# Seven chained block products for x @ w1 and x @ w2 in place of seven for the output, in a fused attention and feed-forward kernel on one core

## The chip, the core and the metric

The kernel runs on one core of a Trainium2 chip. The metric is the device time of one execution in microseconds (us). Engines: TensorE (PE; its weight loads are PEld) multiplies matrices from SBUF into PSUM, which has eight banks of 128 x 512 float32; VectorE (DVE), ScalarE (ACT) and GpSimd (POOL) work on elements; SP only issues DMAs. POOL issues DMAs too.

## The reference

Attention in linear form (8 batches, 8 heads, 576 tokens, head size 64), and its output, as x of 4608 tokens by 512, goes through a multiplicative feed-forward network:

```python
def phi(x, c, s):
    r = np.maximum(x, 0.0)
    return np.concatenate([r * c, r * s], axis=-1)
q_p = phi(q, cos_w, sin_w)
k_p = phi(k, cos_w, sin_w)
kv = np.einsum('bhsf,bhsd->bhfd', k_p, v)
num = np.einsum('bhsf,bhfd->bhsd', q_p, kv)
den = np.einsum('bhsf,bhf->bhs', q_p, np.sum(k_p, axis=2))[..., None] + 1e-06
x = (num / den).transpose(0, 2, 1, 3).reshape(4608, 512)
a = x @ w1          # 512 x 1024
b = x @ w2          # 512 x 1024
h = a * b @ w3      # 1024 x 1024
return h @ w_out    # 1024 x 512
```

w3 @ w_out is formed once on the chip (w34b, 1024 x 512), so each token needs x @ w1, x @ w2, the product a*b and (a*b) @ w34. All products are in bfloat16 with float32 sums.

## The kernel before

The order of everything is written out by hand. PLAN is a string of steps, one line for one step of the feed-forward network and what goes with it: "f t" advances tile t (512 tokens; nine of them) by one step, "k b c", "q b c" and "v b c" make the features and values of chunk c of batch b, "kv b" multiplies keys by values, "n b c" the numerators, "d b c" divides (norm), "xd" and "qd" are DMA transposes on SP's queue, the "l..." steps are loads on POOL's queue (some behind a gate, a one-column copy on POOL that waits for a named result), "st" and "ss" are output stores on POOL's and SP's queues. Each engine works through its own instructions in the order of the plan; a scheduler does not move them.

In a feed-forward tile (ffn_groups) TensorE forms a bank of x @ w1 (L702), ScalarE casts it to asb (L745, L762), TensorE forms the bank of x @ w2, and VectorE multiplies the two into abT (L752, L768). That is 64 matmuls of 512 columns, or twice as many of 256 where a tile goes by halves (BY_HALF). There are four PSUM banks for the network, handed out by turns by a pool, and two more ("more") shortly before the end; the others belong to attention.

Tiles 2 to 7 (SEVEN) form their output (a*b) @ w34 as seven block products in place of eight (seven_products, L895): abT is split in 2 x 2 blocks of 256 tokens by 512 columns and w34 in 2 x 2 blocks. VectorE makes sums of abT blocks (sums, L875) and, once, of weight blocks (weight_block, step "tw"), and additions of the products (L903); ScalarE copies two of them (L914, L917). Tile 8 does this for half of its tokens (small_products), tiles 0 and 1 form the output whole. Outputs wait in twelve buffers of 128 x 2 x 512 for their store.

## Time and profile before

| | |
|---|---|
| times of three runs | 242.2, 242.9, 244.04 us; median 242.9 |
| span of the profiled execution, first to last instruction | 240.1 us (its time with what lies around the span is not given apart) |
| TensorE busy, share | 232.5 us, 97% |
| weight loads busy | 163.0 us, 68% |
| VectorE, ScalarE, POOL busy | 190.8, 115.9, 81.9 us |
| granted TensorE clock | 1.00 throughout |
| moved by DMA | 40.48 MB, mean 169 GB/s |

The span is what the profiler records between the first and the last instruction of one execution; the times are of other executions and include what lies before and after, so they are compared with each other, and spans with spans. A busy TensorE is not one at its peak, since matmuls overlap: the mean of one is 379 ns for 512 columns, where four start within 0.86 us. The page lists for each group of instructions the line, the engine, the names out<-in, the shape, the count, then the busy time and the mean of one.

### The profile page before, as it was taken

How to read it: one execution, taken by the hardware profiler on the slowest of the kernel's cores; microseconds unless marked ns; L12 is line 12 of the kernel's file. 1: busy time of each engine (PE TensorE's matmuls, PEld its weight loads, DVE VectorE, ACT ScalarE, POOL GpSimd, SP SyncE). 2: the span in 40 equal slices, each digit the busy share in tenths (PEclk: the TensorE clock that was granted, in tenths of full speed). 3: DMA queues.
4: the chain of work that ended last, by engine and by line, in shares of the span. 5: the costliest groups of instructions: out<-in, count | busy, mean ns of one | idle time of the engine just before them, and what ended most of it. 6: DMA issues, size and time to landing. Idle time of an engine off the chain costs nothing.

```text
span 240.1 us, 5794 instructions
## 1 busy us (share of the span) xinstructions
PE 232.5 (97%) x2216; PEld 163.0 (68%) x2236; DVE 190.8 (79%) x461; ACT 115.9 (48%) x204; POOL 81.9 (34%) x151
## 2 busy tenths in 40 slices
PE   8899999999999999999999999999999999999993
PEld 3579545567965595798589859966995798484462
DVE  6974586968978947999799889998999788785460
ACT  2853304787755732776384437447164312313321
POOL 8744887761803231221430222021020050372020
PEclk9999999999999999999999999999999999999999
DMA  6999999999999999799999999788456938599924
GB/s 191 197 197 199 187 193 184 199 192 195 186 168 141 145 153 212 99 180 184 164 176 172 143 155 168 128 130 84 77 199 129 115 81 156 127 298 308 278 80 176
DMA packets 85995, 40.48 MB, mean 169 GB/s; under 512 B 49616, under 2 KB 83152, under 8 KB 85968
## 3 DMA queue, kind: packets, MB, share of 16 engines
q0 software_dynamic: 38672, 23.60, 66.9%
q1 hardware_dynamic: 47152, 16.46, 40.7%
q8 instruction: 17, 0.28, 0.5%
q14 instruction: 10, 0.08, 0.1%
q10 hardware_dynamic: 144, 0.07, 0.1%
HBM read 38.80 MB, written 9.44 MB: 201 GB/s over the span
## 4 chain that ended last, share of the span: by engine, by line
PE 92%; DMA 3%; POOL 1%; issue 1%; ACT 1%; DVE 1%; POOLq 0%; DVEq 0%
PE ffnps L702 52%; PE ffnps L895 14%; PE ffnps L785 6%; PE ffnps L498 6%; PE pnum L612 4%; PE pnum L577 4%; DMA vs<-in_v_dram 3%; PE ffnmore L895 1%; PE pst L594 1%; PE ffnps L828 1%; PE ffnps L803 1%; PE pst L654 1%; POOL kf L390 1%; PE pnum L973 0%; ACT qpT L598 0%
## 5 line engine op out<-in xcount | busy, mean ns | idle before, releaser
L702 PE MATMUL ffnps<-xT,w2b 128*128 128x256 bf16 (+2 forms) x448 | 76.2, 303 | 0.1
L702 PE MATMUL ffnps<-xT,w1b 128*128 128x256 bf16 (+2 forms) x435 | 75.1, 301 | 0.7
L702 PEld LDWEIGHTS <-w1b 128*128 128x128 bf16 x448 | 41.1, 98 | 19.3 <-issue 0.8
L702 PEld LDWEIGHTS <-w2b 128*128 128x128 bf16 x448 | 40.7, 98 | 19.7 <-issue 0.2
L762 ACT CAST asb<-ffnps 128x512 bf16<-128x512 f32 x40 | 23.4, 586 | 43.2 <-PE ffnps L702 39.3
L768 DVE TENSOR_TENSOR abT<-asb,ffnps 128x512 bf16<-128x512 bf16 x40 | 27.2, 683 | 15.1 <-PE ffnps L702 14.7
L745 ACT CAST asb<-ffnps 128x512 bf16<-128x512 f32 x24 | 14.1, 586 | 32.9 <-PE ffnps L702 25.9
L625 DVE TENSOR_TENSOR xblk<-pnum,den 128x512 bf16<-128x512 f32 (+1 forms) x38 | 26.2, 691 | 1.5
L526 ACT ACTIVATE kp<-kf,sinv 128x512 bf16<-128x512 bf16 (+4 forms) x33 | 21.0, 663 | 0.9 <-DMA kf<-in_k_dram 0.9
L752 DVE TENSOR_TENSOR abT<-asb,ffnps 128x512 bf16<-128x512 bf16 x24 | 16.2, 681 | 6.5 <-PE ffnps L702 6.5
L895 PEld LDWEIGHTS <-abT 128*128 128x128 bf16 x192 | 18.5, 98 | 3.2
L526 ACT ACTIVATE qp<-qs,sinv 128x512 bf16<-128x512 bf16 (+6 forms) x31 | 18.8, 631 | 2.8 <-DMA qpT<-qp 1.2
L441 POOL COPY seen<-asb 128x1 bf16<-128x1 bf16 x15 | 2.9, 191 | 50.1 <-ACT asb L745 45.3
L612 PEld LDWEIGHTS <-qpT 128*128 128x128 bf16 x320 | 15.0, 98 | 4.6 <-DVE xblk L625 0.6
L785 PE MATMUL ffnps<-w34b,abT 128*128 128x512 bf16 x68 | 16.8, 379 | 0.2
L612 PE MATMUL pnum<-kvs,qpT 128*128 128x65 bf16 x304 | 15.7, 194 | 0.2
L895 PEld LDWEIGHTS <-s 128*128 128x128 bf16 x144 | 14.0, 98 | 1.6
L521 DVE TENSOR_SCALAR kp<-kf,cosv 128x512 bf16<-128x512 bf16 (+1 forms) x40 | 14.8, 391 | 0.2 <-DMA kf<-in_k_dram 0.2
L498 PE MATMUL ffnps<-early,w3T 128*128 128x512 bf16 x62 | 14.2, 379 | 0.1
L521 DVE TENSOR_SCALAR qp<-qs,cosv 128x512 bf16<-128x512 bf16 (+1 forms) x34 | 12.7, 384 | 0.3 <-DMA qs<-in_q_dram 0.2
L895 PE MATMUL ffnps<-w34b,abT 128*128 128x256 bf16 x96 | 12.4, 273 | 0.0
L488 DVE STREAM_TRANSPOSE w3T<-early 128x512 bf16<-128x512 bf16 (+1 forms) x12 | 9.9, 864 | 3.0 <-DMA early<-in_moe_w_dram 3.0
(149 smaller groups left out, 336.6 us busy)
## 6 DMA issues: line engine op xcount, KB each, us to landing
out_dram<-osb SPq DMA_DIRECT2D x9, 256.0 KB, 3.4
kf<-in_k_dram POOLq DMA_DIRECT2D x7, 320.0 KB, 7.8
early<-in_moe_w_dram POOLq DMA_DIRECT2D x16, 128.0 KB, 5.1
vs<-in_v_dram POOLq DMA_DIRECT2D x6, 320.0 KB, 7.2
kf<-in_k_dram POOLq DMA_DIRECT2D x7, 256.0 KB, 8.5
qs<-in_q_dram POOLq DMA_DIRECT2D x5, 320.0 KB, 6.7
qs<-in_q_dram POOLq DMA_DIRECT2D x6, 256.0 KB, 6.3
vs<-in_v_dram POOLq DMA_DIRECT2D x6, 256.0 KB, 8.1
```

The source lines that it names most:

```text
L498: nc.tensor.matmul(acc[:, :], lhsT=w3T[:, lc, :], rhs=woutb[:, lc, :], start=(lc == 0), stop=(lc == 7))
L521: nc.vector.tensor_scalar(out=dst[:R, c, :, 0:D], in0=rows[:R], scalar1=0.0, scalar2=cosv[:R, at:at + 1], op0=ALU.max, op1=ALU.mult)
L526: nc.scalar.activation(out=dst[:R, c, 0:n, D:F], in_=rows[:R, 0:n], func=ACTF.Relu, scale=sinv[:R, at:at + 1], bias=0.0)
L612: nc.tensor.matmul(nt[:, h // 4, ds((h % 4) * 65, 65)], lhsT=qpT[:, h, ds(at, 128)], rhs=kvs[:, h, :], start=True, stop=True)
L625: nc.vector.tensor_tensor(out=xblk[rows, g0:g0 + ng], in0=n4[:, :, :, 0:D], in1=den[rows, 0:ng].unsqueeze(3).to_broadcast([R, ng, 4, D]), ...
L702: nc.tensor.matmul(out, lhsT=w[:, kc, ts(jc, 128)], rhs=x[:, kc, tok], start=(kc == 0), stop=(kc == 3))
L745: nc.scalar.copy(out=asb[:], in_=aT[:, :])
L752: nc.vector.tensor_mul(out=abT[:, ts(pair, 2), ts(half, 256)], in0=asb[:].rearrange("p (i n) -> p i n", i=2), in1=bT[:, :].rearrange("p (i ...
L762: nc.scalar.copy(out=asb[:], in_=aT[:, :])
L768: nc.vector.tensor_mul(out=abT[:, jc, :], in0=asb[:], in1=bT[:, :])
L785: nc.tensor.matmul(ops[:, :], lhsT=abT[:, jc, ts(ms, 128)], rhs=w34b[:, jc, :], start=(jc == 0), stop=(jc == 7))
L895: nc.tensor.matmul(into[:, ts(ms, 256)], lhsT=a[:, kc, ts(ms, 128)], rhs=b[:, kc, :], start=(ms == 0 and kc == 0), stop=(ms == 1 and kc == 3))
```

## The change

The seven products move from the output to the front of the tile. In tiles 3 to 8 (FAST) x @ w1 and x @ w2 are taken together as one product of a 2 x 2 block matrix (x split in two blocks of 256 tokens by two of 256 columns) and a 2 x 2 block matrix (rows 0 to 255 and 256 to 511 of w1 and w2). A pass handles 512 of the 1024 columns, in units u of two column blocks; a tile has two passes of seven products, each on two banks (fast_units, step). Products are chained: 1, 6, 5 and 3 go into one bank x[u] one after the other, 7 and 4 into one bank z[u], and between them ScalarE copies the sum so far out (m1, u1, m7, c12) or VectorE adds to it on its way out (c21, c22). Product 2 has a bank of its own (c11). The blocks c11 to c22 are a and b, and the steps "h" multiply them in bfloat16 into the hidden tile. VectorE forms four sums of x blocks a tile ("xs") and, once, four sums of weights ("tf"); the third overwrites part of w2, so no tile after 2 could use w2 as it was.

The output of all tiles is formed whole (whole_out); in fast tiles it is a generator of its own with steps "o", which the plan sets between the "f" steps of the next tile. Banks are handed out by an explicit list, with six for the network from tile 3 on (more_banks moves up; attention keeps one pair). There are nine output buffers in place of twelve, and tile 2 goes whole. All steps of PLAN stand anew: tiles 3 to 8, and in smaller measure the loads, features and copies of attention.

```diff
-MORE = 8
+MORE = 5
-f 3; k 4 4; k 4 2
 ...
+o 2; xs 3 1 V; v 4 0 A; k 4 1 8; xs 3 3 V
+o 2; qd 4 4
+f 3; tf 1 V; d 3 3; tf 3 V; v 5 1 G; qd 4 3; tf 2 V; more; qd 4 2; xs 3 2 V; v 5 2 G; tf 4 V; lt 5 q 1; xs 3 4 V
 ...
-SEVEN = (2, 3, 4, 5, 6, 7)
-BY_HALF = {t: (1, 0) if t == 3 else (0, 1) for t in range(2, 8)}
-ON_POOL = (8,)
+FAST = (3, 4, 5, 6, 7, 8)
+BY_HALF = {2: (0, 1)}
 ...
+    parts = const.tile([P, 6, 512], FP32, name="parts")
+    sides = const.tile([P, 8, 512], BF16, name="sides")
 ...
     def ffn_tile():
-        return ffn_pool[0].tile([P, 512], FP32, name="ffnps")
+        free.append(free[0])
+        return free.pop(0)
+
+    def keep_bank():
+        return free.pop(0)
 ...
+    W11, W12, W21, W22 = (w[:, ts(r, 2), :] for r in range(2) for w in (w1b, w2b))
 ...
+    def ffn_weight_sum(i, on):
+        t1, t2, t3, t4 = wsum
+        out, a, b = ((t1, W12, W11), (t2, W22, t1), (t3, W22, W12), (t4, W21, t2))[i - 1]
+        on.tensor_tensor(out=out, in0=a, in1=b, op=ALU.subtract)
 ...
+    def x_sum(t, i, on):
+        s1, s2, s3, s4 = xsums
+        a11, a12, a21, a22 = (x_block(t, r, c) for r in range(2) for c in range(2))
+        out, a, b, op = ((s1, a21, a22, ALU.add), (s2, s1, a11, ALU.subtract), (s3, a11, a21, ALU.subtract),
+                         (s4, a12, s2, ALU.subtract))[i - 1]
+        on.tensor_tensor(out=out, in0=a, in1=b, op=op)
+
+    def fast_units(t):
+        (s1, s2, s3, s4), (t1, t2, t3, t4) = xsums, wsum
+        a11, a12, a21, a22 = (x_block(t, r, c) for r in range(2) for c in range(2))
+        factors = {1: (W11, a11), 2: (W21, a12), 3: (W22, s4), 4: (t4, a22), 5: (t1, s1), 6: (t2, s2), 7: (t3, s3)}
+        abT = h_of[t] = Hidden(t)
+        m7, u1, m1 = (parts[:, ts(i, 2)] for i in range(3))
+        c11, c12, c21, c22 = (sides[:, ts(i, 2)] for i in range(4))
+        x, z = {}, {}
+
+        def product(into, u, m, first=True):
+            w, a = factors[m]
+            for i in range(2):
+                for kc in range(2):
+                    nc.tensor.matmul(into[:, ts(i, 256)], lhsT=w[:, kc, ts(2 * u + i, 128)], rhs=a[:, kc, :],
+                                     start=(first and i == 0 and kc == 0), stop=(i == 1 and kc == 1),
+                                     skip_group_check=not first)
+
+        def step(p, m):
+            for j in range(2):
+                u = 2 * p + j
+                if m == 1:
+                    x[u] = keep_bank()
+                    product(x[u], u, 1)
+                    nc.scalar.copy(out=m1[:, j], in_=x[u][:, :])
+                    newest[0] = m1[:, j]
+                elif m == 7:
+                    z[u] = keep_bank()
+                    product(z[u], u, 7)
+                    nc.scalar.copy(out=m7[:, j], in_=z[u][:, :])
+                elif m == 6:
+                    product(x[u], u, 6, False)
+                    nc.scalar.copy(out=u1[:, j], in_=x[u][:, :])
+                elif m == 4:
+                    product(z[u], u, 4, False)
+                    nc.vector.tensor_tensor(out=c21[:, j], in0=z[u][:, :], in1=u1[:, j], op=ALU.add)
+                    free.append(z[u])
+                elif m == 2:
+                    y = ffn_tile()
+                    product(y, u, 2)
+                    nc.vector.tensor_tensor(out=c11[:, j], in0=y[:, :], in1=m1[:, j], op=ALU.add)
+                elif m == 5:
+                    product(x[u], u, 5, False)
+                    nc.vector.tensor_tensor(out=c22[:, j], in0=x[u][:, :], in1=m7[:, j], op=ALU.add)
+                elif m == 3:
+                    product(x[u], u, 3, False)
+                    nc.scalar.copy(out=c12[:, j], in_=x[u][:, :])
+                    free.append(x[u])
+
+        def combine(p, r, on):
+            a, b = ((c11, c12), (c21, c22))[r]
+            on.tensor_mul(out=abT.at(4 * p, 4, ts(r, 256)), in0=a.rearrange("p n (i m) -> p (n i) m", i=2),
+                                 in1=b.rearrange("p n (i m) -> p (n i) m", i=2))
+
+        finish[t] = combine
+        for p, m in ((0, 1), (0, 7), (0, 6), (0, 4), (0, 2), (0, 5), (1, 1), (1, 7), (0, 3), (1, 6), (1, 4), (1, 2), (1, 5), (1, 3)):
+            step(p, m)
+            yield
```

What the change does to the order shows best on three engines. On VectorE, before, the additions of an output (L903) in a tile with attention between them; osb and s are output and side buffers, qp and kp features, den and xblk the division:

```order
L903 TENSOR_TENSOR osb_83<-ffnps,osb_82 128x2x256
L903 TENSOR_TENSOR s_1478<-ffnps,osb_83 128x512
L521 TENSOR_SCALAR qp_93<-qs,cosv 128x8x64
L903 TENSOR_TENSOR osb_82<-ffnps,osb_82 128x2x256
L903 TENSOR_TENSOR s_1479<-osb_83 128x512
L903 TENSOR_TENSOR osb_83<-ffnps,s_1479 128x2x256
L903 TENSOR_TENSOR osb_82<-ffnps,s_1478 128x2x256
L903 TENSOR_TENSOR osb_83<-osb_83,s_1478 128x2x256
```

On VectorE now, the first pass of tile 4, with the additions of products 4 (L896), 2 (L901) and 5 (L904), each for two banks, and the two products of a and b (L912):

```order
L896 TENSOR_TENSOR sides<-ffnps_409,parts 128x512
L896 TENSOR_TENSOR sides<-ffnps_408,parts 128x512
L510 TENSOR_SCALAR qp_92<-qs,cosv 128x8x64
L618 TENSOR_SCALAR den<-pnum 128x8
L619 RECIPROCAL den<-den 128x8
L620 TENSOR_TENSOR xblk<-pnum,den 128x512
L901 TENSOR_TENSOR sides<-ffnps_407,parts 128x512
L901 TENSOR_TENSOR sides<-ffnps_409,parts 128x512
L904 TENSOR_TENSOR sides<-ffnmore_1702,parts 128x512
L904 TENSOR_TENSOR sides<-ffnmore_1703,parts 128x512
```

Before, TensorE waited for such an addition only when the bank came round again; now product 3 goes into the very banks that the last two rows read.

On ScalarE, before, a stretch of one tile, where four casts in a row serve four banks and the features stand between tiles:

```order
L526 ACTIVATE qp_93<-qs,sinv 128x8x64
L762 CAST asb<-ffnps 128x512 x4
L526 ACTIVATE kp_92<-kf,sinv 64x8x64
L914 COPY osb_86<-ffnps 128x2x256
L917 COPY osb_87<-ffnps 128x2x256
L542 COPY va_94<-vs 128x8x64
```

On ScalarE now, the first pass of tile 5: the copies of products 1 (L885), 7 (L890) and 6 (L893), the copy of keys by values (kvs), and features of batches 7 and 6 behind them:

```order
L885 COPY parts<-ffnps_408 128x512
L885 COPY parts<-ffnps_407 128x512
L576 CAST kvs<-pnum 128x520
L890 COPY parts<-ffnps_409 128x512
L890 COPY parts<-ffnps_410 128x512
L893 COPY parts<-ffnps_408 128x512
L893 COPY parts<-ffnps_407 128x512
L515 ACTIVATE kp_91<-kf,sinv 128x6x64
L515 ACTIVATE kp_91<-kf,sinv 128x4x64
L515 ACTIVATE qp_92<-qs,sinv 128x8x64
L515 ACTIVATE qp_92<-qs,sinv 64x4x64
L885 COPY parts<-ffnps_409 128x512
```

The last row is the second pass's product 1: a feature that waits for its load holds it. Every copy of product 1, 7 and 6 is now waited for by a later product into the same bank.

At the seam between tile 2 and tile 3, VectorE now has the sums of x blocks (L859) and of weights (L844) with a division between them, ahead of the first additions:

```order
L859 TENSOR_TENSOR early<-xT 128x512
L510 TENSOR_SCALAR kp_91<-kf,cosv 128x8x64
L859 TENSOR_TENSOR early<-xT 128x512
L844 TENSOR_TENSOR turned<-w2b,w1b 128x2048
L618 TENSOR_SCALAR den<-pnum 128x8
L619 RECIPROCAL den<-den 128x8
L620 TENSOR_TENSOR xblk<-pnum,den 128x512
L844 TENSOR_TENSOR w2b<-w2b 128x2048
L844 TENSOR_TENSOR turned<-w2b,turned 128x2048
L859 TENSOR_TENSOR early<-early,xT 128x512
L844 TENSOR_TENSOR early<-w1b,turned 128x2048
L859 TENSOR_TENSOR early<-xT,early 128x512
```

Before, the weight sums of the old scheme (step "tw") stood one by one in tiles 1 and 2.

More of the change, by code (lines that the diff above doesn't have):

```diff
@@ L697, in new_abT @@
         def new_abT():
[L698 removed]
+            h_of[t] = Hidden(t)
+            return h_of[t]
         def products(out, w, jc, tok):
@@ L724, in on_half @@
                             yield
[L725 to L726 removed]
+                asb = next_side()
+                nc.scalar.copy(out=asb, in_=a[:, :])
                 newest[0] = asb
[L728 to L729 removed]
+                nc.vector.tensor_mul(out=abT.at(2 * pair, 2, ts(half, 256)),
+                                     in0=asb.rearrange("p (i n) -> p i n", i=2),
                                      in1=b[:, :].rearrange("p (i n) -> p i n", i=2))
                 yield
[L733 to L734 removed]
+        if t in FAST:
+            yield from fast_units(t)
+            return
         if t <= 1:
@@ L797, in ffn_groups @@
-        if small:
-            for at, n, copy, queue in ((0, 384, nc.scalar.copy, nc.sync),
-                                       (384, 128, nc.vector.tensor_copy, nc.scalar)):
-                cols = ds(at, n)
-                ops = ffn_tile()
-                for jc in range(8):
-                    nc.tensor.matmul(ops[:, 0:n], lhsT=abT[:, jc, ts(3, 128)],
-                                     rhs=w34b[:, jc, cols], start=(jc == 0), stop=(jc == 7))
-                copy(out=osb[:, 1, cols], in_=ops[:, 0:n])
-                store(queue, osb[:, 1:2, :], 4 * t + 3, 1, cols)
-                yield
```

602 lines of the change are left out of this document (251 added, 351 removed).

## The prediction

> **What bounds the kernel now.** I read the page's engine table first, then the chain that ended last, then the waits of TensorE alone, then the windows of the middle tiles.
>
> ```profile
> span 240.1 us, 5794 instructions
> PE 232.5 (97%) x2216; PEld 163.0 (68%) x2236; DVE 190.8 (79%) x461; ACT 115.9 (48%) x204; POOL 81.9 (34%) x151
> PE 92%; DMA 3%; POOL 1%; issue 1%; ACT 1%; DVE 1%; POOLq 0%; DVEq 0%
> PE unread L481 <- DVE zeros L457: 1.2, 1, 1.2
> PE kva L973 <- DVE kp L521: 0.6, 1, 0.6
> PE pst L594 <- ACT qp L526: 0.3, 1, 0.3
> PE pnum L973 <- DMA vs<-in_v_dram: 0.2, 1, 0.2
> 98.90:188.80 89.90, 89.53 (x908) 69.24 (x913) 82.02 (x200) 49.32 (x88) 18.03 (x36) 1.00 1.04 145
> ```
>
> The chain is TensorE for 92%, and the four rows of its waits (total, times, longest) are all there are: none belongs to the feed-forward network. In the window of tiles 3 to 6 (its columns are length, then busy time of PE, PEld, DVE, ACT, POOL, then clock, DMA share, GB/s) TensorE is busy 89.53 of 89.90 us at clock 1.00 and VectorE 82.02. So the time is the sum of TensorE's work, with nothing to win in waits and everything to lose in new ones; VectorE at 91% is the engine that could make them.
>
> The run shown has a span of 240.1 us; the median of the three times is 242.9, 2.8 above it. I work on the span and add 2.8.
>
> **TensorE's work.** Prices are start to start, from pieces of the chain:
>
> ```profile
> 77.24 3.45 PE ffnps L785 x16
> 100.05 5.24 PE ffnps L895 x48
> 50.17 1.27 PE pnum L577 x40
> 80.69 0.26 PE pnum L612 x8
> ```
>
> A 512-column matmul is 3.45/16 = 0.2156 us and a 256-column one 5.24/48 = 0.1092, so halving the width costs only 1%. Per tile of 512 tokens, in units of 0.2156: x @ w1 and x @ w2 whole are 64, as seven block products 7/8 of that, 56; the output is 32 whole, 28 as seven. Tile 2 goes from 64 + 28 to 64 + 32, tiles 3 to 7 from 92 to 56 + 32 = 88, and tile 8, which split only half its output, from 94 to 88: +4 - 20 - 6 = -22 units. Counted by width: 812 matmuls of 256 columns become 800 (12 x 0.1092 = 1.31) and 392 of 512 columns (or their 384 + 128 pairs) become 376 (16 x 0.2156 = 3.45). **TensorE loses 4.76 us**; attention's matmuls are the same in number. The chained sums add onto a bank that was begun one or two products earlier. No row shows that for these shapes; the nearest are the 65-column products: those of keys and values return to their bank for each of five chunks, 1.27/40 = 0.032 us, and the numerators, which don't add onto anything, take 0.26/8 = 0.033. I take nothing for it; a repeated bank that cost 5% on the 480 later matmuls would be +2.6.
>
> **Semaphores on TensorE.** An instruction with more waits than it can hold gets a semaphore instruction in front:
>
> ```profile
> L702 PEldq EVENT_SEMAPHORE  x13: 51/51/51, 16.2 to 214.1; - x13
> ```
>
> Waits beyond the first on one instruction rise from 40 to 54, mostly loads of qpT and of the first product's weights. 14 x 0.051 = 0.7 us if none hides, 0 if all do. I take **+0.6**, since the chain of before shows pieces of 0.05 "issue" of just this kind.
>
> **VectorE and ScalarE.** Rows for the price of each kind, start to start:
>
> ```profile
> 148.19 0.69 DVE L903 TENSOR_TENSOR osb<-ffnps,osb 128x512 f32<-128x512 f32 x1
> 148.80 0.68 DVE L903 TENSOR_TENSOR s<-osb 128x512 f32<-128x512 f32 x1
> 149.40 0.35 DVE L521 TENSOR_SCALAR kp<-kf,cosv 128x512 bf16<-128x512 bf16 x1
> 144.96 0.42 DVE L875 TENSOR_TENSOR abT<-abT 128x512 bf16<-128x512 bf16 x1
> 145.29 0.68 DVE L875 TENSOR_TENSOR s<-abT,s 128x1024 bf16<-128x1024 bf16 x1
> 145.90 0.34 DVE L521 TENSOR_SCALAR kp<-kf,cosv 64x512 bf16<-64x512 bf16 x1
> 145.57 0.59 ACT L917 COPY osb<-ffnps 128x512 f32<-128x512 f32 x1 [0.29 <-PE ffnps L895]
> 146.05 0.62 ACT L542 COPY va<-vs 128x512 bf16<-128x512 bf16 x1
> ```
>
> An addition of 512 columns with a PSUM or float32 operand holds VectorE 0.60 us, a bfloat16 one of 512 columns 0.33 and of 1024 columns 0.61; a copy out of PSUM holds ScalarE 0.48. VectorE loses 48 products a*b (28.8), the sums of the old scheme (36 large ones, 15.3; small ones and weight blocks, 5.4) and 42 output additions (25.2), together 74.7. It gains 72 additions of chained products (43.2), 24 products of 1024 columns (14.6), 24 sums of x blocks (7.9) and four sums of weights, 128x2048, which no row shows: twice the 1024-column price at most, 1.2, and 0.61 + 2 x 0.28 = 1.15 by the slope; 4.6 for all. Together 70.3. VectorE thus becomes a little lighter, by 4 us and by 11 copies of V that go to POOL and ScalarE. ScalarE loses 48 casts and 14 output copies and gains 96 copies and 26 output copies: +60 x 0.48 = +29 us, to some 145 of 238, 61%. Neither engine is full; what counts is order.
>
> **One pass, by hand.** Two more prices: how long after a bank's last matmul a reader starts, and a division of attention on VectorE (three instructions).
>
> ```profile
> 181.90 1.03 PE L702 MATMUL ffnps<-xT,w1b 128*128 128x512 bf16 x4
> 182.97 0.59 ACT L762 CAST asb<-ffnps 128x512 bf16<-128x512 f32 x1 [0.59 <-PE ffnps L702]
> 152.83 0.16 DVE L623 TENSOR_SCALAR den<-pnum 128x8 f32<-128x8 f32 x1
> 153.94 0.34 DVE L521 TENSOR_SCALAR kp<-kf,cosv 128x512 bf16<-128x512 bf16 x1
> ```
>
> The copy starts at 182.97, 0.2 after 181.90 + 4 x 0.2156, and lasts 0.59; the division holds VectorE 153.94 - 152.83 = 1.1. A product of two banks is 8 x 0.1092 = 0.87 us of TensorE. A tile has two passes; product numbers are those of factors, in tile 5, with T = 0 at the start of product 7.
>
> - TensorE: 7 to 0.87, 6 to 1.75, 4 to 2.62, 2 to 3.49, 5 to 4.37, a numerator 0.26, 1' to 5.5, 7' to 6.4, then 3 at 6.4.
> - ScalarE: the copy of keys by values at 0.2, copies of 7 at 0.7 and 1.2, of 6 at 1.7 and 2.2 (done 2.3 and 2.8).
> - Product 4 needs the first copy of 7 (done 1.3) at 1.75: 0.4 to spare.
> - VectorE: additions of 4 at 2.4 and 3.0, of 2 at 3.6 and 4.2, of 5 at 4.8 and 5.4 (done 5.5, 6.1).
> - 1' reuses 4's bank (free 3.1) at 4.6; 7' reuses 2's (free 4.3) at 5.5; 3 needs 5's additions at 6.4 and 6.8: 0.7 to spare.
>
> Three products give VectorE 3 x 1.21 us in 3 x 0.87 us of TensorE, so it falls 1.0 behind and needs the copy-free products 1' and 7' (and an output step or a numerator) to catch up; the order gives them each time. The tightest places are 0.1 to 0.5 us: product 4 behind the copies of 7, and the last additions of a pass if a division of attention (1.1 us) stands in front. Between the first additions of one pass and of the next, from start-to-start prices, TensorE has 7.9, 7.5, 6.6 and 7.7 us in tiles 3 to 6 where VectorE has 8.0, 7.3, 7.0 and 6.8, and 14 us against 11.5 to 12.6 in the other half. Level, then ample. At the seam of tile 3 the four weight sums, four x sums and a division (some 7 us) run under the eight output steps of tile 2 (8 x 0.86): 1.2 us to spare.
>
> I take **+1.0** for all new waits: about 60 places with 0.1 to 0.7 us to spare, of which a late division or a slow VectorE instruction will spoil some. Below: 0. Above: the rivals.
>
> The loads move too. The products of keys and values of batches 5 to 7 stand 7 to 8 us earlier against the tiles than before, and their loads stand earlier with them. SP's and POOL's stores of tiles 0 to 4 now stand between loads and copies of V; they wait for data long finished, so they cost POOL's issue time alone, and ScalarE's reuse of an output buffer (nine now, twelve before) comes 8 us or more after its store.
>
> The end is as before: two output blocks, the last cut in 384 and 128 columns, and
>
> ```profile
> 234.52 1.76 PE ffnps L803 x16
> 236.31 0.29 DVE osb L805
> ```
>
> so 3.8 us from the last matmul to the end of the span stay.
>
> **Sum:** 240.1 - 4.76 + 0.6 + 1.0 = 236.9 span, + 2.8 = **239.7 us**. Its own range, with waits from 0 to 3: 238.1 to 241.7.
>
> **Rivals.**
>
> *VectorE late in every pass (slower).* The additions of 5 stand behind a division in each pass; with 1.1 us in front and 0.4 to spare, product 3 waits 0.7, twelve times 8.4 us. That gives 242.9 - 4.76 + 8.4 = **246.5**. It decides from 0.4 us a pass on. For it speak the 91% of VectorE; against it that it was as busy before without one wait of TensorE, and that in tiles 7 and 8, which have little attention, nothing stands in front.
>
> *Loads late.* ScalarE's keys of a batch stand between copies that product 4 needs, in one queue; a late load holds them all.
>
> ```profile
> kf<-in_k_dram POOLq DMA_DIRECT2D x7, 256.0 KB, 8.5
> DMA to landing us min/median/max: 4.6/7.9/10.8
> ```
>
> In tile 3 I count 8.6 us from the issue of the second half of batch 5's keys to their use and 9.2 for batch 4's. At the longest landing, 10.8 us, ScalarE stands 2 us and TensorE 1.4. In three batches 4.2: 239.7 + 4.2 - 1.0 = **242.9**, no change.
>
> *POOL against VectorE.* Copies of V on POOL rise from 9 to 17.
>
> ```profile
> 46.71 1.89 POOL L390 DMA_DIRECT2D qs<-in_q_dram  x1 [0.24 <-DMA kf<-in_k_dram]
> 47.98 1.39 DVE L521 TENSOR_SCALAR kp<-kf,cosv 128x512 bf16<-128x512 bf16 x2
> L542 POOL COPY va<-vs 128x512 bf16<-128x512 bf16 x6 | 3.8, 639 | 6.9 <-DMA vs<-in_v_dram 6.9
> ```
>
> Here a DMA issue on POOL took 1.89 us and, beside it, two VectorE instructions 1.39 together in place of 0.6: each delayed the other. If each of the 17 copies holds VectorE for its 0.64 us, that is 5 us more than before by eight copies, half of it in the level stretches: +2.6, **242.3**, no change. The Trainium skill's SBUF — State Buffer, Who interferes with whom, has this as a lock: VectorE shares one port pair with GpSimd, and whoever starts first keeps it for its whole instruction. By that rule the new two-operand sums, all in SBUF, would be hit and the additions out of PSUM not; the two rows agree, though they do not show which instruction held what. By that rule the sum would be the 242.3 above; by the nine copies of before, beside which TensorE waits for nothing, it stays 239.7.
>
> **Chances.** The forecast 0.58; VectorE late 0.17; loads late 0.15; POOL against VectorE 0.10. A difference of about 1% (2.4 us) is what a measurement of this kernel can tell from none. Nine tenths of the forecast lie below 240.5, 0.52, and with a little of the middle rivals faster has 0.57. Within 1% (240.5 to 245.3): the rest of the forecast, most of the middle rivals and the milder part of the first, 0.27. Slower: most of the first, and late loads that are worse than counted, 0.16. The range must leave out no more than 2 in 10: it reaches from 238.0 (no new wait, most semaphores hidden) to 245.2, past the two middle rivals and into the first.
>
> **What would show it.** Right: TensorE's chain share stays near 92%, and its busy time falls by 4 to 5 us; the group of 672 chained matmuls has 273 ns each; waits of TensorE on VectorE and ScalarE sum to under 2 us, spread thin; VectorE's busy time falls by 3 to 8 us; ScalarE's rises by some 30. Wrong: single waits of TensorE on sides or parts above 0.5 us in each pass (first rival); ScalarE waiting for kf, qs or vs loads by 2 us at a time, followed by TensorE (second); VectorE's short instructions lengthened beside POOL's copies (third). A saving of TensorE's work below 4 us would mean that chained sums are not free.

## The result

The changed kernel takes **257.6 us** (median of four runs, 255.98 to 260.93) against 242.9: ratio 1.059, interval 1.052 to 1.066. Slower by 14.6 us, where 239.7 (238.0 to 245.2) was forecast. The slower rival, 246.5, falls short too. The profiled execution took 256.15 us, with a span of 254.3. Ratios here and below leave out executions more than 1.5% above the fastest of the same kernel, medians leave out none.

The page of the changed kernel: busy times, TensorE and the granted clock in 40 slices, and the chain that ended last.

```profile
span 254.3 us, 5749 instructions
PE 232.8 (92%) x2208; PEld 160.5 (63%) x2208; DVE 184.5 (73%) x436; ACT 143.5 (56%) x262; POOL 87.1 (34%) x157
PE   8799999899999999979699995799779899999993
PEclk9999999999999999999799999999999999999999
PE 44%; DMA 31%; DVE 13%; POOL 4%; issue 3%; SPq 2%; ACT 1%; DVEq 0%; POOLq 0%
```

TensorE was 92% of the chain and is 44%; DMA was 3% and is 31%. The stretch that before had TensorE busy for 89.53 of 89.90 us ran from the start of tile 2's output to the start of tile 6's. These now come at 103.1 and 203.2 us, and the row below begins 4 us before the first (columns as there):

```profile
98.90:203.00 104.10, 92.45 (x892) 66.94 (x891) 85.08 (x195) 65.22 (x123) 36.64 (x65) 0.98 1.10 177
```

11.65 us of it TensorE is idle, and the clock fell to 0.98. What it waited for (total, times, longest), the five largest of rows that sum to 16.9 where before's summed to 2.3:

```profile
PE pnum L607 <- DMA qpT<-qp: 4.3, 3, 3.1
PE pnum L607 <- DVE xblk L620: 1.9, 1, 1.9
PE ffnmore L875 <- DVE early L859: 1.6, 1, 1.6
PE ffnps L875 <- DMA xT<-xblk: 1.4, 1, 1.4
PE ffnmore L804 <- DVE abT L912: 1.3, 1, 1.3
```

These are not many thin waits but single ones of 1 to 3 us, most of them for a DMA transpose or for what stands behind one (the sums "early" at L859 are x sums, made from the transposed xT). The largest, at 156 us, read backwards: the transpose of batch 5, chunk 1, on SP, and the numerators on TensorE that need it; before first, then the change.

```profile
133.75 1.23 SPq L550 DMA_TRANSPOSE qpT<-qp  x1
150.87 0.42 PE L612 MATMUL pnum<-kvs,qpT 128*128 128x65 bf16 x8
```

```profile
148.61 2.87 SPq L539 DMA_TRANSPOSE qpT<-qp  x1
159.19 0.43 PE L607 MATMUL pnum<-kvs,qpT 128*128 128x65 bf16 x8 [3.15 <-DMA qpT<-qp]
```

Before, it was issued 17.1 us ahead of its use. Now the use would have come 7.4 us after the issue (10.6 with the 3.15 of waiting), and the transpose took 10.5 to land. Beside it, in the same 8 us, POOL's queue has loads and output stores side by side:

```profile
144.26 0.90 POOL L389 DMA_DIRECT2D kf<-in_k_dram  x1 [0.32 <-issue]
145.15 1.12 POOL L682 DMA_DIRECT2D out_dram<-early  x2
147.40 0.91 POOL L389 DMA_DIRECT2D vs<-in_v_dram  x1
150.04 0.89 POOL L389 DMA_DIRECT2D qs<-in_q_dram  x1
151.59 1.11 POOL L682 DMA_DIRECT2D out_dram<-early  x2
```

In the kernel before, nearly all stores on POOL came behind the last load:

```profile
194.96 3.17 POOL L687 DMA_DIRECT2D out_dram<-early  x6 [0.28 <-issue]
208.47 4.17 POOL L687 DMA_DIRECT2D out_dram<-osb  x8 [0.28 <-issue]
```

The step "st" waits for nothing but its data, and POOL runs far ahead of the plan: the store issued from 151.59 on belongs to a row that TensorE reaches at 167.5 us. The loads are bunched too: before, batch 7's six large loads were issued from 140.8 to 162.6 us, and now five of them from 144.3 to 150.9.

Pairing all transposes of features after 75 us with their numerators (25 of them): the time from issue to use was 13.6 us in the median and 7.6 at least, with landings of 4.4 (median) to 9.0. In the change it is 12.4 and 3.5 (waits included), with landings of 6.0 (median) to 11.4. So **leads shrank and landings grew**. Shortest lead and longest landing belong to different transposes: before, 7.6 against 9.0 cost no wait, and in the change the one with a lead of 3.5 landed in 3.3. Three of the 25 landed too late; they are the three waits of the first row above.

### The profile page after: what moved, and what is told of

Same layout as the page of the kernel before. It is cut to its first block, busy times and chain, and to the rows that moved or that the text cites. A ratio compares the mean times of both kernels' runs of the same rounds, so it can differ in the third digit from the quotient of the medians.

```text
span 254.3 us, 5749 instructions
## 1 busy us (share of the span) xinstructions
PE 232.8 (92%) x2208; PEld 160.5 (63%) x2208; DVE 184.5 (73%) x436; ACT 143.5 (56%) x262; POOL 87.1 (34%) x157
## 4 chain that ended last, share of the span: by engine, by line
PE 44%; DMA 31%; DVE 13%; POOL 4%; issue 3%; SPq 2%; ACT 1%; DVEq 0%; POOLq 0%
DMA xT<-xblk 14%; PE ffnps L875 13%; PE ffnps L804 10%; PE ffnmore L875 8%; DMA kf<-in_k_dram 7%; PE ffnps L723 6%; DMA w2b<-in_moe_w_dram 4%; DMA qpT<-qp 4%; PE ffnmore L804 3%; PE pnum L572 3%; DVE xblk L620 2%; PE pnum L607 2%; DMA early<-in_moe_w_dram 2%; POOL early L417 2%; SPq L539 1%
## 5 line engine op out<-in xcount | busy, mean ns | idle before, releaser
L804 PE MATMUL ffnps<-w34b,abT 128*128 128x512 bf16 (+1 forms) x224 | 52.3, 377 | 0.0
L723 PE MATMUL ffnps<-xT,w1b 128*128 128x128 bf16 (+2 forms) x176 | 26.8, 282 | 0.4 <-DMA xT<-xblk 0.3
L723 PE MATMUL ffnps<-xT,w2b 128*128 128x128 bf16 (+2 forms) x176 | 26.8, 282 | 0.2 <-DVE abT L788 0.2
L607 PEld LDWEIGHTS <-qpT 128*128 128x128 bf16 x320 | 14.6, 98 | 13.2 <-DMA qpT<-qp 4.7
L912 DVE TENSOR_TENSOR abT<-sides 128x1024 bf16<-128x1024 bf16 x24 | 17.6, 734 | 7.0 <-ACT sides L907 6.9
L875 PEld LDWEIGHTS <-turned 128*128 128x128 bf16 x192 | 18.8, 99 | 3.6 <-DVE early L859 1.1
L515 ACT ACTIVATE kp<-kf,sinv 128x512 bf16<-128x512 bf16 (+5 forms) x30 | 18.8, 661 | 1.1 <-DMA kf<-in_k_dram 1.1
L875 PE MATMUL ffnps<-xT,w1b 128*128 128x256 bf16 x136 | 17.7, 273 | 1.4 <-DMA xT<-xblk 1.4
L804 PE MATMUL ffnmore<-w34b,abT 128*128 128x512 bf16 (+1 forms) x72 | 16.2, 361 | 1.3 <-DVE abT L912 1.3
L875 PE MATMUL ffnps<-early,turned 128*128 128x256 bf16 x128 | 16.6, 273 | 0.8 <-DVE early L859 0.8
L875 PE MATMUL ffnps<-early,w2b 128*128 128x256 bf16 x120 | 15.4, 273 | 0.0
```

Of the source, the lines that this page charges most:

```text
L515: nc.scalar.activation(out=dst[:R, c, 0:n, D:F], in_=rows[:R, 0:n], func=ACTF.Relu, scale=sinv[:R, at:at + 1], bias=0.0)
L607: nc.tensor.matmul(nt[:, h // 4, ds((h % 4) * 65, 65)], lhsT=qpT[:, h, ds(at, 128)], rhs=kvs[:, h, :], start=True, stop=True)
L723: nc.tensor.matmul(out, lhsT=w[:, kc, ts(jc, 128)], rhs=x[:, kc, tok], start=(kc == 0), stop=(kc == 3))
L804: nc.tensor.matmul(banks[ms, at][:, 0:n], lhsT=abT.one(jc, ts(ms, 128)), rhs=w34b[:, jc, ds(at, n)], start=(jc == 0), stop=(jc == 7))
L875: nc.tensor.matmul(into[:, ts(i, 256)], lhsT=w[:, kc, ts(2 * u + i, 128)], rhs=a[:, kc, :], start=(first and i == 0 and kc == 0), stop=(i ...
L912: on.tensor_mul(out=abT.at(4 * p, 4, ts(r, 256)), in0=a.rearrange("p n (i m) -> p (n i) m", i=2), in1=b.rearrange("p n (i m) -> p (n i) m" ...
```

## The experiments

Medians in us; before was 242.2 to 242.5 beside each of them. In PLAN, "st" is an ungated store on POOL's queue, "sg" and "sx" are stores gated behind TensorE's newest product copy or newest transpose. Theory A at the start: the stores among the loads make the transposes late. Rival B: late key features and POOL's copies of V at the seam of tile 3. In the expectations, theory B is VectorE behind in each pass, and theory C the loads, not the stores.

**e1: stores later.** Nine of the steps "st" from tile 4 on become gated ones, most of them further down, for instance:

```diff
-o 3; xd 4 4; n 5 4; d 5 4; xd 5 4; st; st; h 4 0 1 V
+o 3; xd 4 4; n 5 4; d 5 4; xd 5 4; st; h 4 0 1 V
-f 5; qd 6 4; st; qd 6 2
+f 5; qd 6 4; sg; sg; qd 6 2
```

> Against the changed kernel (256 to 259 us). What is altered: POOL's second store waits with the third for the first product of tile 5, the fourth and fifth for that of tile 6, and three more are put behind the keys by values of batch 7. Theory A (stores that POOL issues ungated at 145 to 156 and 173 to 190 us stand before the DMA transposes in the DMA engines, and these land late, 8 to 11 us after their issue in place of 3 to 4): the waits of 3.15, 1.38, 1.63 and 0.78 us go, and most of the 1.31 behind POOL: 6 to 8 us off, 249 to 251. Theory B (VectorE is behind in each pass whatever lands): at most 1 us off. Theory C (the loads, not the stores, make the transposes late): at most 2 us off, the 3.15 and 1.38 stay.

Measured 260.3 (256.95 to 264.55), no better. (The profiled execution took 264.55, above the median, so its waits are on the long side.)

```profile
PE pnum L607 <- DMA qpT<-qp: 14.6, 3, 7.2
162.49 0.62 PE L607 MATMUL pnum<-kvs,qpT 128*128 128x65 bf16 x8 [7.17 <-DMA qpT<-qp]
```

The same numerators now wait 7.2 us: the transpose of batch 5, chunk 1, is issued at 151.0, 2.4 us later than in the change, and batch 7's loads, issued from 144 to 151, are still beside it; it lands after 11.5. Stores that were moved to 198–202 us met another transpose (6.2 us of waiting). Theory A alone falls.

**e2, e3: the seam.** e2 moves one key feature step two rows down; e3 also moves three copies of V off POOL's row of weight sums.

```diff
-f 3; qd 4 0; xd 3 3; kv 4; k 5 1 4
+f 3; qd 4 0; xd 3 3; kv 4
-f 3; k 5 3 8; q 5 0 8; d 4 1; h 3 0 0 V; lg 6 q 1
+f 3; k 5 1 4; k 5 3 8; q 5 0 8; d 4 1; h 3 0 0 V; lg 6 q 1
```

> Only the features of chunk 1 of batch 5's keys are moved, behind the division of chunk 0 of batch 4, in the queues of VectorE and ScalarE. Theory A2 (these features wait for a load that lands at 120.9 us and hold the division of which the second numerator waits 1.92 us, and the half clock of 3.4 us follows from that idle time): 1.9 + 1.7 = 3.6 us off, 253 to 254. Theory B (VectorE is too full there): the wait stays under another name, 0 to 1 us off.

> The same, and three copies of V of batch 5 on POOL are moved behind the weight sums of tile 3 on VectorE. If POOL's copies lengthen VectorE's sums (1.63 in place of 1.22 us twice, 0.83 for 0.42, 0.70 for 0.34, 0.60 for 0.25): about 1.5 us more off than with the keys alone, 251.5 to 252.5, and the two waits of 0.78 and 0.51 us at the start of tile 3 go. If they do not matter: the same as with the keys alone.

Measured 259.6 (256.7 to 260.2) and 257.7 (256.2 to 260.0). The edit did what it should, and the time did not follow:

```profile
123.34 0.42 PE L607 MATMUL pnum<-kvs,qpT 128*128 128x65 bf16 x8 [0.44 <-DVE xblk L620]
PE pnum L607 <- DMA qpT<-qp: 8.7, 3, 4.5
PE ffnps L723 <- DMA xT<-xblk: 3.6, 1, 3.6
```

The wait of 1.92 became 0.44 and others grew by more. Moving the copies took away the 0.78 and 0.51 in front of the weight sums, again without a gain. **e4** joins e1 and e3:

> All three edits together. If theories A and A2 and the contention with POOL are the causes, they add: 257 - 7 - 3.6 - 1.3 = 245, within 2. If the waits only go elsewhere (theory B): 252 or more.

Measured 261.0 (257.4 to 262.9). Single answers do not add up.

**e5, e6: fewer loads in flight.** From batch 4 on each load is gated on the landing of the one two before it (e5); e6 adds the seam edits of e3, later loads of batch 7 and stores spread out, and leaves one pair of output blocks unwritten.

```diff
+    landing = lambda b, mark: [b >= 4 and len(sent) >= 2 and gate(sent[-2]), b >= 4 and sent.append(mark)]
-                nc.gpsimd.dma_start(out=t[:, :, 0:4, :].rearrange("p h j d -> p h (j d)"),
+                landing(b, t[:, 0, 0, 0:1]); nc.gpsimd.dma_start(out=t[:, :, 0:4, :].rearrange("p h j d -> p h (j d)"),
```

> From batch 4 on, POOL issues a load only when the load two before it has landed (one small copy on POOL as its gate), so that no more than two are in the DMA engines at once; the stores stay as they are. Theory C (bunches of four to six loads, issued within 3 to 7 us at 79, 124 and 144 us, make the transposes issued behind them land 9 to 12 us later in place of 3 to 6): the wait at 90 to 93 us (0.3 to 3.6 us by run) and the one at 156 to 160 (3.2 and more) shrink to under 1.5 us together; 4 to 6 us off, 251 to 253. Theory A (stores): at most 1 us off. Rival: loads that start later make features late, and the waits only change their name: 0 or slower.

> No more than two loads at once, the queries of batch 7 loaded behind the first product of tile 5, the stores at places where few transposes run (two behind the first product of tile 5, two behind its second pass, the others behind the transposes of batch 7), and the two edits at tile 3 (features of batch 5's keys later, three copies of V later). If bunched transfers and the seam of tile 3 are the whole loss: waits fall from 15 to some 4 us and the time to 243 to 246. If the order of VectorE's work is what binds: 252 or more.

Measured 258.9 (258.0 to 260.5) and 254.1 (253.1 to 255.0). In e5 the waits at 90 and 156 us are gone, and others come in their place: 4.67 behind late key features, 3.03 behind an output copy for which ScalarE waited 5.7 us until a store had freed the buffer, and 2.49 for an x sum behind its transpose.

**e7, e8: take the traffic away.** e7 loads a sliver of batch 7 and reuses batch 5's data (first two lines); e8 issues no store on POOL's queue (last).

```diff
-            raw[b, name] = kbufs[b % 2] if name == "k" else ...
+            raw[b, name] = raw[5, name] if b == 7 else kbufs[b % 2] if name == "k" else ...
...
-        store(nc.gpsimd, osb[:, :, :], g, 2)
```

> The loads of batch 7 are left out but for 64 rows of 128x8x64 of each tensor (192 KB in place of 1.7 MB; its attention then uses rows of batch 5); stores stay. Theory C: the transposes issued at 147 to 156 us land 3 to 5 us after their issue and the waits at 156 to 163 us (3.15 and 1.38 us in the changed kernel) go: 3.5 to 5 us off. Theory A: these waits stay at 3 us or more, since the stores at 145 to 156 us remain.

> POOL's stores of whole outputs are left out (11 of the pairs of output blocks of tiles 0 to 7, some 5.5 MB); loads stay. Theory A: the waits at 156 to 163 and at 181 to 199 us go, 7 us off. Theory C: the wait at 156 to 160 us stays at 3 us or more, and only those after 180 us (1.3, 1.6 and 0.8 us, where nothing but stores runs beside the transposes) go: 3 us off. With both left out of the account in turn, the two losses should add up to the DMA waits of the changed kernel, 7.6 us.

e7: 255.3 (247.2 to 256.4). Its times give no verdict: the profiled execution is the one of 247.2, and the other three took 255 or more. But its trace answers for the chunk at 156 us. With batch 7's loads gone and the stores still beside it, the transpose lands 4.9 us after its issue, and the numerators wait for nothing:

```profile
144.25 1.37 SPq L539 DMA_TRANSPOSE qpT<-qp  x1
150.97 0.42 PE L607 MATMUL pnum<-kvs,qpT 128*128 128x65 bf16 x8
```

e8: **248.6** (247.5 to 251.9), ratio 1.021. So POOL's stores take part in some 9 us of the loss, after e1 had shown that moving them gives nothing. In e8:

```profile
PE pnum L607 <- DMA qpT<-qp: 2.0, 1, 2.0
xT<-xblk SPq DMA_TRANSPOSE x31, 4.3
qpT<-qp SPq DMA_TRANSPOSE x30, 4.4
```

Landings are near those of before in the median (rows of DMA issues: count, median us to landing), but the chunk at 156 us still waits 2.0: beside batch 7's loads it takes 9.7 us to land, and its numerators would have come 7.8 us after its issue. So at this chunk the loads decide, as theory C said, and the stores after it: of features issued from 165 to 185 us the slowest took 11.4 us in the change, 12.0 in e7 and 4.6 in e8.

**e9: weight sums earlier**, three of four among tile 2's steps.

```diff
+f 2; tf 1 V; qd 3 4; n 3 0; d 3 0; q 3 2 8
+f 2; tf 2 V; qd 3 3
+f 2; tf 4 V; xd 3 0; q 4 4 0
-f 3; tf 1 V; d 3 3; tf 3 V; v 5 1 G; qd 4 3; tf 2 V; more; qd 4 2; xs 3 2 V; v 5 2 G; tf 4 V; lt 5 q 1; xs 3 4 V
+f 3; d 3 3; tf 3 V; v 5 1 G; qd 4 3; more; qd 4 2; xs 3 2 V; v 5 2 G; lt 5 q 1; xs 3 4 V
```

> One edit in the changed kernel: three of the four sums of weights (those that don't overwrite a weight) are placed in tile 2, where VectorE is half idle, in place of the start of tile 3. If VectorE's work at that seam (four sums of 1.1 to 1.5 us, an x sum that waits for its transpose ahead of them) causes the waits of 0.78 and 0.51 us there: these two go, and VectorE reaches the division before the second numerator earlier, but the late keys still hold it: 1.3 to 2 us off, 255.5 to 256.5. If it is the transposes of x alone: the same time.

Measured 261.5 (256.5 to 262.5). The waits of 0.78 and 0.51 are gone, with nothing won.

**e10, e11, e12: all of it together**, with the edits of e3 and e9, stores spread and loads moved, for instance as below; e11 adds e5's gates, e12 is e11 without POOL's stores.

```diff
-f 1; l 3 k 1; v 3 3 V
+f 1; l 3 k 1; st; st; v 3 3 V
-f 2; l 5 v 1; v 5 3 G; n 3 2
+f 2; l 5 k 1; n 3 2
-f 5
+f 5; lg 7 q 0; l 7 q 1
```

> All that the runs so far point to: three weight sums in tile 2; the second half of batch 5's keys loaded ahead of its V, and its features and four copies of V later; the queries of batch 7 loaded behind the first product of tile 5; the two stores of tile 0 in tile 1 (about 66 us), the next three behind products of tiles 5 and 6, the others behind the last transposes. Theory (bunched transfers ahead of the transposes, and the seam of tile 3): waits of TensorE after 45 us fall from 14 to 4 or 5 us, 244 to 247. Rival (VectorE's order inside the passes): 251 or more.

> The same, and from batch 4 on no more than two loads in flight. The bunch of four loads at 79 to 82 us is the one that is left in the kernel before this: without it the wait for the transposes of x at 90 to 93 us (0.3 to 3.6 us, by run) goes, 242 to 245. If late loads cost as much as the bunch: 244 to 248.

> The same with POOL's stores left out (12 pairs of output blocks are not written). What is left of the waits then comes from loads, the seam and VectorE. If the new places of the stores do no harm: within 1.5 us of the kernel with them. If stores anywhere before 200 us still delay transposes: 3 us or more faster, near 240.

Measured 256.4 (253.7 to 265.3), 259.0 (251.1 to 261.6), 249.1 (247.3 to 250.6). Times that spread over 11 us suggested that it depends on which transposes meet which traffic, so I turned to the leads.

**e13: leads only.** Five transposes (the expectation says six) move up in SP's queue (xd 2 2, qd 5 1, xd 4 3, xd 5 0, qd 7 4), for instance:

```diff
-f 4; q 5 3 8; qd 5 3; n 5 0; d 5 0; lx 7 k 0
+f 4; q 5 3 8; qd 5 3; qd 5 1; n 5 0; d 5 0; lx 7 k 0
-o 3; xd 4 4; n 5 4; d 5 4; xd 5 4; st; st; h 4 0 1 V
+o 3; xd 4 4; xd 4 3; xd 5 0; n 5 4; d 5 4; xd 5 4; st; st; h 4 0 1 V
```

> In the changed kernel only the place of six DMA transposes in SP's queue is altered: each is issued right behind the instruction that makes its data (features of batch 5 chunk 1, of batch 7 chunk 4; blocks of x of batch 2 chunk 2, batch 4 chunk 3, batch 5 chunk 0), with all loads and stores as they are. Theory D (the new order gives the transposes too little lead: by the trace of before every feature is issued 7.6 us or more ahead of its numerator and lands in at most 9.0; in the changed kernel the shortest leads are 3.5 to 7 us and landings reach 11.4): the waits at 90, 156 to 163 and 198 us shrink by 5 us in all, 250 to 253. If traffic alone decides, an earlier issue only waits longer: 256 to 258.

Measured 257.4 (255.6 to 259.3), no better. The waits at 90 and 156 us are gone, but later transposes, beside the stores at 173 to 190 us, are late:

```profile
185.51 0.59 PE L607 MATMUL pnum<-kvs,qpT 128*128 128x65 bf16 x8 [3.06 <-DMA qpT<-qp]
191.50 0.72 PE L875 MATMUL ffnmore<-early,w2b 128*128 128x256 bf16 x5 [2.18 <-DVE early L859]
```

**e14: leads and everything else**: e13's rows, those of e3 and e9, stores spread as in e18 below, and batch 4's second half of V loaded later.

```diff
-f 2; l 4 v 1; v 4 2 G; lk 5 k 0; v 4 4 A; q 3 4 2
+f 2; lk 5 k 0; v 4 4 A; q 3 4 2
```

> The earlier transposes together with the weight sums in tile 2, the keys of batch 5 ahead of its V, later V copies, one store at 66 us, three behind the first products of tile 5, one behind tile 6's, the others behind the last transposes. If the leads, the bunches and the seam are the loss: waits after 45 us of 3 us or less, 241 to 244. If the DMA engines are simply full until 180 us, so that each transfer that is moved hits another transpose: 248 or more.

Measured **246.9** (245.3 to 249.0), ratio 1.016.

**e15: almost no traffic after 125 us**: no stores on POOL, and batches 6 and 7 reuse earlier data.

```diff
+            raw[b, name] = raw[b - 2, name] if b >= 6 else kbufs[b % 2] if name == "k" else ...
...
-        store(nc.gpsimd, osb[:, :, :], g, 2)
```

> The changed kernel with its order untouched, without POOL's stores and without the loads of batches 6 and 7 but for 64 rows of each tensor of batch 7 (attention then uses rows of batches 4 and 5, and 12 pairs of output blocks are not written). If transfers are the cause of the waits after 125 us, whatever the order of VectorE's and ScalarE's work: waits only at 50, 70, 90 to 93 and 112 to 124 us, 6 us or less, and 243 to 246. If VectorE or ScalarE is behind in the passes of tiles 4 to 6: waits of sides and parts of 2 us or more remain after 125 us, 248 or more.

Measured 245.8 (244.7 to 248.1). Transposes land after 2.9 and 4.0 us, and what is left of the waits named above is

```profile
PE pnum L607 <- DVE xblk L620: 1.8, 1, 1.8
PE ffnmore L804 <- DVE abT L912: 0.2, 1, 0.2
```

The first is the seam of tile 3, at 122 us. After 125 us the second is the only wait of TensorE at all. So from tile 4 on the passes as I worked them out by hand run without a wait of 0.2 us or more when nothing comes late, and "VectorE late in every pass" falls.

**e16: the other way round.** The kernel before, with its eight gated or late stores on POOL as early as in the change:

```diff
-f 4; d 5 0; lx 7 k 0
+f 4; d 5 0; lx 7 k 0; st; st
-f 5; n 5 2; k 7 2; k 7 1; k 7 0 4; lg 7 v 1; qd 6 0
+f 5; n 5 2; k 7 2; k 7 1; k 7 0 4; lg 7 v 1; st; st; st; st; st; qd 6 0
```

> The kernel before, with eight of POOL's stores placed as the changed kernel has them: two behind the first load of batch 7's keys, one behind its queries, five behind the last load of its V. If early stores alone delay the transposes beyond their leads: 2 to 5 us slower than before, 244.5 to 247.5. If before's longer leads (7.6 us and more) cover it: within 1 us of 242.4, and its transposes land later (over 5 us in the median after 140 us, 3.2 before) without a wait.

Measured 242.6 (ten runs), ratio 1.001, interval 0.998 to 1.003. Its transposes, against before's 4.1 and 5.3:

```profile
xT<-xblk SPq DMA_TRANSPOSE x31, 6.0
qpT<-qp SPq DMA_TRANSPOSE x30, 6.7
```

From 145 to 165 us, where the moved stores begin, transposes of x land after 9.4 us in the median (4.2 before, 9.2 in the change), up to 10.6, and it costs nothing: the features' leads are 7.4 us at least and 12.7 in the median. The loads here are as before, not bunched.

**e17: e14, with its remaining waits answered one by one**, as this one at 122 us:

```diff
-f 3; n 4 0; h 3 0 1 V; d 4 0; lx 6 q 0
+f 3; n 4 0; d 4 0; h 3 0 1 V; lx 6 q 0
```

> From the kernel with all edits (246.9): the numerators of batch 2 one product later behind their keys by values; the transposes of batch 2 chunk 2, batch 3 chunk 2 and batch 6 chunk 4 earlier in SP's queue; divisions of batch 4 ahead of the features and of the combination beside them in tile 3, the query features of batch 5 behind the next product; one copy of a transpose from VectorE to ScalarE. Each answers one wait of 0.4 to 1.0 us in its trace, together 6.1, and each wait ended saves 0.17 us of TensorE's refilling more, 7.6 in all. If leads and order of VectorE's queue are what is left: 240 to 242, faster than before. If each moved instruction delays another: 245 or more.

Measured 247.2 (245.9 to 248.9), no gain: others of 0.9 to 1.4 us came in their place.

**e18: the changed kernel with e13's leads and the stores of e14, and nothing else.**

```diff
-f 1; l 3 k 1; v 3 3 V
+f 1; l 3 k 1; st; v 3 3 V
-f 5; lg 7 v 1
+f 5; lg 7 v 1; sg
-f 7; st; xs 7 3 V; xd 7 3; n 7 2; xs 7 1 V; xs 7 2 V; xs 7 4 V
+f 7; xs 7 3 V; xd 7 3; sx; n 7 2; xs 7 1 V; xs 7 2 V; xs 7 4 V
```

> Of the kernel with all edits (246.9) only two are kept: the earlier issue of six transposes, and the stores' new places; tile 3's seam, the loads and the V copies are as in the changed kernel. Alone, the earlier transposes gave nothing (257.4), and moved stores with a later transposes' order nothing (260.3). If lead and traffic together are the loss (each transfer needs the other's room): 249 to 251, with the waits at 112 to 124 us (3 to 4 us and a half clock) left. If tile 3's seam and the loads had to be mended for the rest to pay: 254 or more.

Measured **246.1** (244.6 to 248.7), ratio 1.018, interval 1.013 to 1.022: 11.4 us less than the change by the medians, some 10 by the ratios, where e13's leads alone gave none. The store places of e18 alone were not run. Those of e1 alone gave nothing, and the nearest is e10, with almost the same store places, the old leads, and the seam's and loads' edits: 253.7 and 253.9 in its two fastest runs, against 246.9 for e14, which has the leads too. e14 also differs in three loads, so this speaks for the leads without proving it. That e18 does as well as e14 says that the seam's edits and moved loads add nothing. Its chain of the disputed chunk (in a group of three transposes), its rows of landings, and its first waits:

```profile
137.43 5.55 SPq L539 DMA_TRANSPOSE qpT<-qp  x3
153.59 0.42 PE L607 MATMUL pnum<-kvs,qpT 128*128 128x65 bf16 x8
xT<-xblk SPq DMA_TRANSPOSE x31, 6.0
qpT<-qp SPq DMA_TRANSPOSE x30, 5.9
PE pnum L607 <- DMA qpT<-qp: 1.3, 2, 1.0
PE pnum L607 <- DVE qpT L593: 1.2, 1, 1.2
```

The transposes still land late, only no longer too late: this chunk, the last of the three, has a lead of some 12 us and no wait. No version beat the kernel before.

## Why the prediction was wrong, and where it was right

Right: the chain of the change shows

```profile
115.50 1.75 PE ffnps L875 x16
203.38 1.73 PE ffnps L804 x8
```

0.109 and 0.216 us each, so adding onto a bank begun earlier cost nothing here, and by count and price the 4.76 us were taken out of TensorE's work. (The matmuls that add onto an earlier product are 384, four products of seven, not 480.) The sign named for it, a busy time 4 to 5 us lower, did not come: 232.8 against 232.5. Busy time also counts half clock and draining matmuls (point 3), and before's record has 20 matmuls fewer than weight loads (2216 and 2236), where the change's has none missing. VectorE lost 6.3 us (forecast 3 to 8), ScalarE gained 27.6 (some 30). Semaphore instructions on TensorE's weight loads rose by 12, from 29 to 41 (14 counted). A weight sum of 128x2048 took 1.22 us where nothing ran beside it (1.15 to 1.2 said).

Wrong, by the steps as put:

1. **"They wait for data long finished, so they cost POOL's issue time alone."** Transposes beside the stores also land later. e8 shows the size, some 9 us; e16 shows the landings rising where stores alone are moved. Bunched loads do the same, as e7 shows at 144 us. The Trainium skill, DMA: Bandwidth & Descriptors, Queues, rings and completion order, says that each DMA engine takes turns between the queues for which it has work; that a transpose on SP's queue is late while POOL's has traffic agrees, 10.5 us above against medians of 2.9 (xT) and 4.0 (qpT) in e15. What share each queue gets, no run shows.

2. **"The loads move too"** compared loads with their uses and stopped there. The same comparison for SP's transposes was missing, and it is the step that failed: the sum put late transposes at nothing, and at 156 us a lead of 7.4 us met a landing of 10.5. Long leads with early stores cost nothing (e16), short leads without stores give back some 9 us (e8), stores moved as in e1 or leads lengthened alone give nothing (e1, e13), leads and e18's store places together some 10 (e18): the price is that of short leads and late landings meeting.

3. **"I take +1.0 for all new waits."** The waits rose by 14.6 us (16.9 less 2.3). Two costs had no term. Each wait loses about 0.17 us more than it shows: eight 256-column matmuls are shown as 1.04 us and take 0.87 start to start, so TensorE counts as busy while its last ones drain; fourteen more waits (18 against 4) make 2.4 by this estimate. And one wait brought half clock, 1.6. The sum is then 240.1 − 4.76 + 14.6 + 2.4 + 1.6 + 0.3 (a longer end) = 254.2, against a span of 254.3; the semaphores, 12 × 0.051 = 0.6 if none hides, are not told apart in it.

4. **"1.2 us to spare" at the seam of tile 3.** Eight steps of 0.86 are 6.9 us, no more than the 7 us of sums set against them, so the spare time did not follow from these numbers. TensorE lost 0.78 and 0.51 waiting for the sums and 1.92 behind them:

```profile
110.88 1.63 DVE L844 TENSOR_TENSOR turned<-w2b,turned 128x2048 bf16<-128x2048 bf16 x1
112.77 1.63 DVE L844 TENSOR_TENSOR early<-w1b,turned 128x2048 bf16<-128x2048 bf16 x1
120.95 0.51 ACT L515 ACTIVATE kp<-kf,sinv 128x256 bf16<-128x256 bf16 x1 [0.92 <-DMA kf<-in_k_dram]
122.49 0.69 DVE L620 TENSOR_TENSOR xblk<-pnum,den 128x512 bf16<-128x512 f32 x1
```

Two sums took 1.63, beside POOL. Then keys landed at 120.9, 7.7 us after their issue at 113.2. That is less than the 8.6 that I had counted from issue to use, but ScalarE stood ready 6.9 us after the issue, and VectorE's division stood behind the features. This is rival "Loads late", in one batch of three and at 1.9.

The rival "POOL against VectorE" exists at a smaller size: lengthened instructions cost VectorE 6.05 us in all, 4.3 before. One of them sits in front of the 1.3 us wait for abT:

```profile
180.12 1.08 DVE L510 TENSOR_SCALAR qp<-qs,cosv 128x512 bf16<-128x512 bf16 x1
181.12 1.09 DVE L912 TENSOR_TENSOR abT<-sides 128x1024 bf16<-128x1024 bf16 x1
180.98 1.05 POOL L682 DMA_DIRECT2D out_dram<-q0f  x2
```

Alone they take 0.34 and 0.68. In e1 the stores are not there, and that wait is 0.16.

Open: e18 is 8.6 us over the 237.5 that 242.26 less 4.76 would give. In its profile, 7.5 over, the shown waits make 4.2 (6.5 less 2.3), seven more refills 1.2 and the semaphores at most 0.6. Another 1.3 is chance: full clock began 7.2 us after the start of the span, 4.6 in before's profile, and the first twenty matmuls took 7.45 us in place of 6.16. So the saved 4.76 us are there, and waits and their refills cost 5.4; e17 shows that taking them one by one brings others. Even without the traffic (e15, 245.8) the change is no faster than before. That nine output buffers in place of twelve force stores among the loads is argued from the plan; a version with twelve wasn't tried.

## What to carry to other kernels

When a reordering moves DMAs, list for each transfer that TensorE waits on how long before its use it is issued, and compare that with the longest landing in the stretch where it runs, not with the median. A lead at or above it is safe; a shorter one may still be in time, as here. A store whose data is ready is not free: on a queue that runs ahead it goes out early and can delay what others wait for, and so can loads issued in a bunch. In a kernel with one engine at 97%, a saving of 2% in that engine's work is a loss if it eats the slack of the transfers.

## What the runs showed of the hardware

**A wait of 2 us can halve the clock for 3.4.** The windows of the change around the waits at 121 and 156 us (columns as above; the first number behind the length is TensorE's busy time, the granted clock is third from the end):

```profile
120.25:123.66 3.41, 1.49 (x26) 1.17 (x23) 2.60 (x8) 2.44 (x5) 0.19 (x1) 1.00 0.68 84
123.66:127.07 3.41, 3.41 (x20) 2.45 (x17) 2.39 (x6) 2.15 (x4) 3.29 (x8) 0.50 0.58 55
154.38:157.79 3.41, 1.67 (x8) 0.57 (x6) 2.71 (x9) 2.95 (x6) 0.53 (x1) 1.00 1.46 157
157.79:161.21 3.42, 2.02 (x17) 1.08 (x18) 1.06 (x3) 0.00 (x0) 0.00 (x0) 1.00 1.39 182
```

1.92 us inside one window (TensorE busy 0.44 of it) brought a whole window at 0.50; 3.15 us split over two brought nothing. Over all traces of this study half clock came in whole 3.41 us steps of one grid, behind windows with TensorE busy under some 0.40: in 20 of 20 at 0.38 or less, in 4 of 6 between 0.40 and 0.45, and in 2 of some 90 between 0.45 and 0.8 (one of the two in the first 9 us, one already at half clock). The price at the same place, twelve output matmuls after a wait of 1.97 us in e8 and after none in e18:

```profile
156.89 4.44 PE L804 MATMUL ffnmore<-w34b,abT 128*128 128x512 bf16 x12
```

```profile
153.85 2.75 PE L804 MATMUL ffnmore<-w34b,abT 128*128 128x512 bf16 x12
```

1.7 us (4.44 less 2.75) for such a window. The Trainium skill, TensorE: Matmul & The Clock Gate, Part 1, gives one idle window of about 3.4 us as what brings the clock down; here a window idle for little more than half was enough.

**POOL lengthens VectorE's SBUF instructions, by its DMA issues too.** All 33 lengthened VectorE instructions (13 before, 20 after) lay beside a POOL instruction, some beside a DMA issue alone, and all had their tensors in SBUF; of the operations that read PSUM (some 190 and 180), about 70 in each kernel lay beside one and none was longer for it. Lying beside POOL is not enough: of some 245 SBUF instructions of VectorE that did, in both traces together, most were not longer. The rule of the Trainium skill's SBUF — State Buffer that the prediction names agrees.
